# A fourth buffer for two tiles' rows of x, and one weight split moved up, in a fused attention and mixture-of-experts kernel

## The chip, the cores and the metric

The kernel runs on one core of a Trainium2 chip. The metric is the device time of one launch in microseconds (us), as the median of the runs shown; lower is better. A profiled execution, with the time of each instruction, stands beside it.

## The reference

Chunked softmax attention first (8 batches, 8 heads, 576 positions, heads of 64, chunks of 64 positions that see only themselves), then a mixture of 8 experts on its output. A token takes the expert that is the argmax of its gate, or, where its local gate is at 0.5 or above, the expert of the token before it:

```python
def _attn_ref(q, k, v):
    B, H, S, D = q.shape                      # 8, 8, 576, 64
    chunk = 64
    nc = S // chunk
    scale = 1.0 / np.sqrt(D)
...
    scores = scale * np.matmul(q_c, k_c.transpose(0, 1, 2, 4, 3))
    scores = scores - np.max(scores, axis=-1, keepdims=True)
    attn = np.exp(scores)
    attn = attn / (np.sum(attn, axis=-1, keepdims=True) + 1e-09)
    out = np.matmul(attn, v_c)
...
def _moe_ref(x, w_gate, w_local, w1, w2):     # w1: 8 x 512 x 1024, w2: 8 x 1024 x 512
    logits = np.einsum('bsd,de->bse', x, w_gate)
    local_gate = 1.0 / (1.0 + np.exp(-np.einsum('bsd,de->bse', x, w_local).squeeze(-1)))
...
            fresh_e = int(np.argmax(logits[b, s]))
            if s == 0 or local_gate[b, s] < 0.5:
                e = fresh_e
            else:
                e = prev_e if prev_e >= 0 else fresh_e
...
            p = np.exp(ls)
            p /= p.sum() + 1e-09
            h = np.maximum(x[b, s] @ w1[e], 0.0)
            out[b, s] = p[e] * (h @ w2[e])
```

x is the attention output with its heads side by side: 4608 tokens of 512.

## The kernel before

**Tiles.** The 4608 tokens are cut into 18 attention tiles of 256 (numbers 0 to 17). A tile goes through these steps: its q and k are loaded by DMA (buffers `qt`, `kt`, three of each; L135) and v (`vbuf`, three buffers until tile 11; L149); GpSimd (POOL) pairs the heads (`qr`, `kr`; L166); TensorE (PE) transposes the pairs into `qT`, `kT` (L174; ScalarE, ACT, copies them out of PSUM, L164); PE makes the scores (`sc`, L204), VectorE (DVE) takes the maximum off (L215, L218), ACT the exponential (`pr`, L223); PE transposes the result to `pT` and multiplies with v (`o`, L253); DVE divides by the sum and writes the rows of x into a buffer `xs` (L267, in two halves). PE transposes `xs` (L174, ACT copies to `xT`, L164) and makes the router's logits (`lg`, L296), which DVE copies (`lT`), PE transposes (L307, L309) and DVE reduces into the last columns of `xs` (L316). Then one DMA (L318) stores the tile from `xs` to `x_d` in DRAM. `xs` comes from a ring of three buffers, so the L267 that starts a tile waits until the store of the tile three before has read its buffer.

**The order.** It is written by hand. A steady loop runs i from 1 to 15 by a string of tokens, each engine in the order in which the instructions are recorded: iteration i has the scores of tile i+1, the transposes of `pr` and the values of tiles i and i-1, the q and k transposes of tile i+2, the pairs of tile i+3 on POOL, the x transposes, the router and the store of tile i-2, and the loads of q and k of tile i+5 and of v of tile i+2. SyncE's queue (SP) issues all loads and the stores to `x_d`, in order, and waits there for what a transfer needs. Behind the loop the last attention tiles are mixed with the first routed ones, and then the experts' matmuls follow.

**The first expert's weights.** w1 of an expert lies in four pieces of 128 x 1024, w2 in four pieces of 128 x 2 x 512. Each is loaded raw (`raw1` in the two buffers `raw_0`, `raw_1`; `raw2` in two more, `pair2[0]` and `pair2[1]`) and then split into a high and a low part: ACT casts to `w1h` (L102), then the low part `w1l` is raw minus high (L103), in this stage on POOL, in two halves of 512 columns. Piece c of w1 is loaded at the end of iteration 9+c and split at the end of iteration 11+c; the four pieces of w2 are loaded at the ends of iterations 13 and 14. Until then the first half of `pair2[0]` is unused, and `pair2[1]` serves as the third buffer of v.

**The first routed tiles.** Behind iteration 14, POOL writes the masks `rh` (L441) from DVE's running counts (L416 to L437, L819), and indirect DMAs (L613) gather the rows of the first experts' tiles into `raw_0` and `raw_1`; PE transposes them (L607) among the last attention tiles.

Of the kernel before, what the change touches and what calls it, by code (L numbers as in the profile page):

```python
# [8 lines left out]
F32 = mybir.dt.float32  # L9
# [12 lines left out]
E, F = 8, 1024  # L22
C = H * D
N = B * S
P = 128
NT = N // P
NS = N // 256
XR = C + E + 1
# [38 lines left out]
def tile_attention_then_moe(ctx: ExitStack, tc, q, k_in, v, wg, wl, w1, w2, out):  # L67
    nc = tc.nc
# [17 lines left out]
    w1h = [wpool.tile([P, F], F32R, name=f"w1h{c}") for c in range(4)]  # L86
    w1l = [wpool.tile([P, F], F32R, name=f"w1l{c}") for c in range(4)]
# [3 lines left out]
    pair2 = [wpool.tile([P, 4, C], F32, name=f"raw2_{g}") for g in range(2)]  # L91
    raw1 = [pair1[c // 2][:, c % 2] for c in range(4)]
    raw2 = [pair2[c // 2][:, c % 2 * 2:c % 2 * 2 + 2] for c in range(4)]

    def load_w1(e, c):
        nc.sync.dma_start(raw1[c], w1[e, P * c:P * c + P, :])

    def load_w2(e, c):
        nc.sync.dma_start(raw2[c], w2[e, 256 * c:256 * c + 256, :].rearrange("(f p) d -> p f d", p=P))

    def split(hi, lo, raw, lo_eng=None):
        nc.scalar.copy(hi, raw)  # L102
        (lo_eng or nc.vector).tensor_tensor(lo, raw, hi.bitcast(F32), ALU.subtract)  # L103
# [5 lines left out]
    pa2 = ctx.enter_context(tc.tile_pool(name="pa2", bufs=2, side="right"))  # L109
# [8 lines left out]
    vbuf = [pa1.tile([P, 2, H, DV], F32, name=f"v{i}") for i in range(2)]  # L118
    vbuf.append(pair2[1].rearrange("p a c -> p (a c)")[:, 0:2 * H * DV].rearrange("p (c h d) -> p c h d", c=2, h=H))
    V3 = 12  # L120

    def cut(i):
        n = -256 * i % S
        return 1 if n == 0 or n >= 256 else 2 if n == 128 else 4
# [16 lines left out]
    def load_v(i):  # L141
        vt = vbuf[i % 3 if i < V3 else i % 2]
        for cp in range(2):
            t0 = 256 * i + P * cp
            while t0 < 256 * i + P * cp + P:
                b, s0 = t0 // S, t0 % S
                n = min(S - s0, 256 * i + P * cp + P - t0)
                p0 = t0 % P
                nc.sync.dma_start(vt[p0:p0 + n, cp, :, 0:D], v[b, :, s0:s0 + n, :].rearrange("h s d -> s h d"))  # L149
                t0 += n  # L150
        return vt
# [92 lines left out]
    def values(pT, vt, xs, fine=False):  # L244
        box = {}

        def group(j, h):
            if h == 0:
                box["o"] = ps_o.tile([P, 2, 512], F32, name="o")
            o = box["o"]  # L250
            for cp in range(2):
                for cc in range(2):
                    nc.tensor.matmul(  # L253
                        o[64 * cp:64 * cp + 64, cc, DV * h:DV * h + D + 1],
                        pT[64 * cc:64 * cc + 64, 4 * j + h, 64 * cp:64 * cp + 64],
                        vt[64 * cc:64 * cc + 64, cp, 4 * j + h, 0:D + 1],
                        start=True, stop=True,
                    )
            if h == 3 and not fine:
                norm(j)  # L260

        def norm(j):
                ov = box["o"][:, :, 0:4 * DV].rearrange("p c (h d) -> p c h d", d=DV)
                rs = pa2.tile([P, 2, 4], F32, name="rs")
                nc.vector.tensor_scalar_add(rs, ov[:, :, :, D], 1e-9)
                nc.vector.reciprocal(rs, rs)
                nc.vector.tensor_tensor(  # L267
                    xs[:, :, 256 * j:256 * j + 256].rearrange("p c (h d) -> p c h d", d=D),
                    ov[:, :, :, 0:D],
                    rs.unsqueeze(3).to_broadcast([P, 2, 4, D]),  # L270
                    ALU.mult,
                )

        out = []
        for j in range(2):
            out += [lambda j=j, h=h: group(j, h) for h in range(4)]
            if fine:
                out.append(lambda j=j: norm(j))
        return out
# [42 lines left out]
    def ok(i):  # L322
        return 0 <= i < NS

    def load_vs(i):
        for n in range(2 if i == 1 else i + 2 - (i > V3), (i + 2 if i < V3 else i + 1) + 1):
            vts[n] = load_v(n)
# [119 lines left out]
    qk, hd, vts, qkT, prs, pTs, xss, xTs = ({} for _ in range(8))  # L447

    def a_tq(i, engs=None):
        qkT[i] = (pe2.tile([P, 4, 256], F32, name="qT", bufs=1), pe2.tile([P, 4, 256], F32, name="kT", bufs=1))  # L450
        return qk_transposes(hd.pop(i), *qkT[i], cut(i), engs)

    def a_pair(i, engs=(nc.gpsimd,) * 4):
        hd[i], fns = pair_heads(qk.pop(i), engs)
        return fns

    def a_sa(i, fine=False):
        prs[i] = pa2.tile([P, H, 2, D], F32, name="pr")
        return scores(*qkT.pop(i), prs[i], fine)

    def a_tp(i, fine=False):
        pTs[i] = pa2.tile([P, H, P], F32, name="pT")
        return p_transposes(prs.pop(i), pTs[i], fine)

    def a_va(i, fine=False):
        xss[i] = pa2.tile([P, 2, XR], F32, name="xs", bufs=3)
        return values(pTs.pop(i), vts.pop(i), xss[i], fine)

    def a_tx(i, fine=False):
        xTs[i] = pa2.tile([P, 4, 256], F32, name="xT", bufs=1)  # L470
        return x_transposes(xss[i], xTs[i], fine)

    def a_ra(i, fine=False):
        return router(i, xTs.pop(i), xss.pop(i), fine)

    def play(order, qs, its=None, more=False):
        its = {} if its is None else its
        for tok in order.split():
            name, _, n = tok.partition("*")
            if name not in its:  # L480
                its[name] = iter(qs[name]())
            for _ in range(int(n or 1)):
                next(its[name])()
        if more:
            return
        for name, it in its.items():
            assert next(it, None) is None, name
        assert set(its) == set(qs), set(qs) - set(its)

    def run(fns):  # L490
        for fn in fns:
            fn()
# [25 lines left out]
    for b in range(B):  # L518
        t, p = divmod(b * S, P)
# [11 lines left out]
    with tc.manual_schedule(engines=MAN):  # L531
        def load(store, fn, i):
            def go():
                store[i] = fn(i)
            return lambda: [go]
# [288 lines left out]
    hooks = {}  # L824
    for fn, at in zip(hq, PAR["hooks"]):
        hooks.setdefault(divmod(at, 4), []).append(fn)
    man = tc.manual_schedule(engines=MAN | {ET.Pool})
    man.__enter__()
    for i in range(1, NS - 2):
        qs4 = dict(s=lambda: a_sa(i + 1), tp=lambda: a_tp(i), va=lambda: a_va(i - 1, True), tq=lambda: a_tq(i + 2))  # L830
        opt = dict(lq=load(qk, load_qk, i + 5) if ok(i + 5) else None,
                   lv=(lambda: [lambda: load_vs(i)]),
                   pr=(lambda: a_pair(i + 3)) if ok(i + 3) else None, tx=(lambda: a_tx(i - 2)) if i >= 2 else None, ra=(lambda: a_ra(i - 2, True)) if i >= 2 else None)
        for h in range(4):
            opt[f"h{h}"] = (lambda h=h: [lambda: run(hooks[i, h])]) if (i, h) in hooks else None
        toks = [t for t in PAR["steady"].split() if opt.get(t.split("*")[0], 1) is not None]
        play(" ".join(toks), qs4 | {k: v for k, v in opt.items() if v is not None})
        if 9 <= i < 13:
            load_w1(0, i - 9)
        if i in (13, 14):  # L840
            for c in range(2 * i - 26, 2 * i - 24):
                load_w2(0, c)
        if 11 <= i < 15:
            for col in (slice(0, 512), slice(512, F)):
                split(w1h[i - 11][:, col], w1l[i - 11][:, col], raw1[i - 11][:, col], nc.gpsimd)

    def w2_split(c):
        return [lambda: nc.scalar.copy(w2h[c], raw2[c]),
# [4 lines left out]
    n = NS - 1  # L853
# [77 lines left out]
    for k, fn in (("tp", a_tp), ("va", a_va), ("tx", a_tx), ("ra", a_ra)):  # L931
        for d in range(5):
            queues[f"{k}{d}"] = lambda fn=fn, d=d: fn(n - d, True)
# [146 lines left out]
    with tc.manual_schedule(engines=MAN | {ET.SP, ET.Pool}):  # L1080
# [5 lines left out]
        for t in range(EARLY, LAST + 1):  # L1086
            step(t)
            n = t - EARLY
# [30 lines left out]
```

## Time and profile before

| | us |
|---|---|
| median of 3 runs | 672.22 (671.09 to 674.7) |
| profiled execution, whole | 675.2 |
| span of the profiled execution, first to last instruction | 673.4 |
| PE busy in the span | 633.6 |

The profiled execution took 675.2 us, of which 673.4 are the span in the trace. The program is 16385 instructions on five engines. The page's slices are 16.8 us each: PE is full from the tenth slice on, and short of full in the slices before, which are the attention stage.

### The profile page before, as it was taken

The page shows a single profiled execution, that of the slowest core. Times are in us where ns is not written, and L with a number is a line of the kernel's source. Part 1 is how long each engine was busy: PE and PEld are TensorE (multiplying, and loading weights), DVE is VectorE, ACT ScalarE, POOL GpSimd, SP SyncE. Part 2 cuts the span into 40 slices and gives each one's busy share as a digit, 9 for nine tenths or more (in the row PEclk, how much of TensorE's full clock was granted, in tenths as well). Part 3 has the DMA queues.
Part 4 walks back from the last instruction along what each step waited for, and adds up shares of the span by engine and source line. Part 5 has one row for each costly group of instructions (what it writes and reads, how often), then busy time and mean ns, then how long its engine had stood idle before and what let it go on. Part 6 is the DMA issues. An engine that isn't in the chain of part 4 may idle for free.

```text
span 673.4 us, 16385 instructions
## 1 busy us (share of the span) xinstructions
PE 633.6 (94%) x5684; PEld 503.2 (75%) x5684; DVE 362.6 (54%) x936; ACT 267.5 (40%) x439; POOL 150.8 (22%) x214
## 2 busy tenths in 40 slices
PE   5899989888999999999999999999999999999993
PEld 4677777666777887778888877788877888768872
DVE  2656667686787376663232466643467422564230
ACT  4657667656322235442122343422454222442220
POOL 5323224472022111211121121221122211212101
PEclk9989999998999999999999999999999999999998
DMA  9999999995614114545111153551148511244101
GB/s 230 249 229 258 236 264 280 301 282 164 236 37 143 33 49 174 177 160 177 35 64 34 33 191 145 191 172 44 38 171 292 176 38 34 66 158 167 48 19 37
DMA packets 102829, 98.23 MB, mean 146 GB/s; under 512 B 42388, under 2 KB 79252, under 8 KB 102676
## 3 DMA queue, kind: packets, MB, share of 16 engines
q1 hardware_dynamic: 88644, 61.01, 32.7%
q0 software_dynamic: 6640, 20.65, 9.2%
q10 hardware_dynamic: 7392, 14.68, 6.2%
q8 instruction: 77, 1.26, 0.8%
q14 instruction: 76, 0.62, 0.3%
HBM read 77.28 MB, written 20.35 MB: 145 GB/s over the span
## 4 chain that ended last, share of the span: by engine, by line
PE 39%; issue 26%; DMA 23%; DVE 5%; SPq 3%; POOL 2%; POOLq 1%; ACT 0%; DVEq 0%
DMA out<-ysb,sidx 14%; PE y L660 12%; PE h L646 12%; DMA x_d<-xs 7%; PE tr L174 4%; SPq L135 3%; PE o L253 2%; PE tr L740 2%; DVE xs L267 2%; PE tr L725 1%; PE y L667 1%; POOL rh L441 1%; DMA qt<-in_q 1%; PE h L654 1%; PE lg L296 1%
## 5 line engine op out<-in xcount | busy, mean ns | idle before, releaser
L660 PE MATMUL y<-w2h,hp 128*128 128x512 f32 x560 | 185.8, 401 | 1.0 <-ACTq L954 1.0
L646 PE MATMUL h<-w1h,xp 128*128 128x512 f32 x560 | 161.6, 398 | 0.0
L775 POOL DMA_INDIRECT out<-ysb,sidx x41 | 41.9, 1021 | 369.9 <-DVE ysb L772 284.3
L660 PEld LDWEIGHTS y<-w2h,hp 128*128 128x128 f32 x560 | 105.2, 188 | 24.8 <-ACTq L954 1.2
L646 PEld LDWEIGHTS h<-w1h,xp 128*128 128x128 f32 x560 | 102.1, 188 | 20.1 <-issue 0.2
L660 PE MATMUL y<-w2l,hp 128*128 128x512 f32 x280 | 110.7, 395 | 0.1
L646 PE MATMUL h<-w1l,xp 128*128 128x512 f32 x280 | 87.3, 393 | 0.4 <-DVEq L954 0.4
L713 ACT CAST hp<-tr 128x512 fp32r<-128x512 f32 x64 | 34.9, 589 | 119.5 <-PE tr L740 116.8
L772 DVE TENSOR_SCALAR ysb<-y,ppr 128x512 f32<-128x512 f32 x35 | 26.3, 750 | 87.4 <-PE y L660 68.1
L646 PEld LDWEIGHTS h<-w1l,xp 128*128 128x128 f32 x280 | 52.5, 188 | 12.4 <-DVEq L954 0.9
L660 PEld LDWEIGHTS y<-w2l,hp 128*128 128x128 f32 x280 | 52.7, 188 | 11.5 <-DVEq L954 0.6
L699 ACT ACTIVATE hsb<-h 128x1024 f32<-128x1024 f32 x35 | 35.9, 1026 | 60.2 <-PE h L646 57.6
L714 DVE TENSOR_TENSOR xp<-tr,xp 128x512 fp32r<-128x512 f32 x32 | 22.1, 690 | 58.9 <-ACTq L954 56.2
L714 DVE TENSOR_TENSOR hp<-tr,hp 128x512 fp32r<-128x512 f32 x64 | 41.6, 685 | 15.5 <-ACT hp L713 13.7
L632 ACT ACTIVATE pex<-pex 128x8 f32<-128x8 f32 x41 | 8.6, 209 | 102.4 <-DVE pex L631 89.1
L613 POOL DMA_INDIRECT xg<-x_d,gidx x39 | 41.4, 1063 | 14.1 <-issue 10.1
L740 PEld LDWEIGHTS tr<-ident,hsb 128*128 128x128 f32 x274 | 31.9, 140 | 9.0 <-ACTq L954 3.3
L740 PE MATMUL tr<-ident,hsb 128*128 128x128 f32 x274 | 37.3, 274 | 1.4 <-DVEq L954 1.4
L103 DVE TENSOR_TENSOR w1l<-raw,w1h 128x1024 fp32r<-128x1024 f32 x28 | 33.0, 1222 | 8.3 <-ACT w1h L102 8.3
L103 DVE TENSOR_TENSOR w2l<-raw,w2h 128x1024 fp32r<-128x1024 f32 x28 | 32.4, 1220 | 3.9 <-ACT w2h L102 3.9
L166 POOL COPY qr<-qt 128x512 f32<-128x512 f32 x34 | 19.9, 613 | 65.3 <-PE tr L174 44.0
L267 DVE TENSOR_TENSOR xs<-o,rs 128x512 f32<-128x512 f32 x36 | 24.9, 693 | 14.5 <-DMA x_d<-xs 13.6
(210 smaller groups left out, 851.5 us busy)
## 6 DMA issues: line engine op xcount, KB each, us to landing
raw<-in_moe_w SPq DMA_DIRECT2D x14, 1024.0 KB
raw<-in_moe_w ACTq DMA_DIRECT2D x14, 1024.0 KB, 6.4
x_d<-xs SPq DMA_DIRECT2D x18, 521.0 KB, 6.0
raw<-in_moe_w SPq DMA_DIRECT2D x16, 512.0 KB
v<-in_v SPq DMA_DIRECT2D x26, 256.0 KB, 7.0
qt<-in_q SPq DMA_DIRECT2D x11, 512.0 KB, 6.5
kt<-in_k SPq DMA_DIRECT2D x11, 512.0 KB, 7.6
qt<-in_q SPq DMA_DIRECT2D x16, 128.0 KB, 3.8
```

What stands on the lines that cost most here:

```text
L103: (lo_eng or nc.vector).tensor_tensor(lo, raw, hi.bitcast(F32), ALU.subtract)
L174: nc.tensor.transpose(box["ps"][:, n], src_of(n), ident)
L267: nc.vector.tensor_tensor(xs[:, :, 256 * j:256 * j + 256].rearrange("p c (h d) -> p c h d", d=D), ov[:, :, :, 0:D], rs.unsqueeze(3).to_bro ...
L613: nc.gpsimd.indirect_dma_start(out=dst, out_offset=None, in_=src, in_offset=bass.IndirectOffsetOnAxis(ap=gidx[t].bitcast(U32), axis=0))
L646: nc.tensor.matmul(hs[:, j], xs[a][:, c], W1[w][c][:, 512 * j:512 * j + 512], start=(c == 0 and n == 0), stop=(c == 3 and n == 2))
L660: nc.tensor.matmul(y, hx[f // 4][a][:, f % 4], W2[w][c][:, f % 2, :], start=(f == 0 and n == 0), stop=(f == 7 and n == 2))
L699: nc.scalar.activation(hsb, hs.rearrange("p j f -> p (j f)"), AF.Relu)
L713: nc.scalar.copy(p[:, 0], ps)
L714: V.tensor_tensor(p[:, 1], ps, p[:, 0].bitcast(F32), ALU.subtract)
L740: nc.tensor.transpose(ps[:, n], hsb[:, at + P * n:at + P * n + P], ident)
L772: either(kind and kind[1], lambda: V.tensor_scalar(ysb, y, pr, None, ALU.mult), lambda: y_part(ysb, y, pr))
L775: nc.gpsimd.indirect_dma_start(out=out, out_offset=bass.IndirectOffsetOnAxis(ap=sidx[t].bitcast(U32), axis=0), in_=ysb, in_offset=None, bo ...
```

## The change

Tiles 3 and 7 write their rows of x not into the ring but into a fourth place, `xs4`, which is the front of the raw w2 buffer `pair2[0]`; the ring of three then serves tiles 0, 1, 2, 4, 5, 6, 8, 9, 10, 11 and so on. The split of w1's piece 3 moves from the end of iteration 14 to the end of iteration 13, behind that of piece 2. The loads stand where they stood.

```diff
     V3 = 12
+    xs4 = pair2[0].rearrange("p a c -> p (a c)")[:, 0:2 * XR].rearrange("p (c n) -> p c n", c=2)
...
     def a_va(i, fine=False):
-        xss[i] = pa2.tile([P, 2, XR], F32, name="xs", bufs=3)
+        xss[i] = xs4 if i in (3, 7) else pa2.tile([P, 2, XR], F32, name="xs", bufs=3)
         return values(pTs.pop(i), vts.pop(i), xss[i], fine)
...
+    def w1_split(c):
+        for col in (slice(0, 512), slice(512, F)):
+            split(w1h[c][:, col], w1l[c][:, col], raw1[c][:, col], nc.gpsimd)
+
+    w1_at = {11: (0,), 12: (1,), 13: (2, 3)}
...
-        if 9 <= i < 13:
-            load_w1(0, i - 9)
+        for c in {9: (0,), 10: (1,), 11: (2,), 12: (3,)}.get(i, ()):
+            load_w1(0, c)
...
-        if 11 <= i < 15:
-            for col in (slice(0, 512), slice(512, F)):
-                split(w1h[i - 11][:, col], w1l[i - 11][:, col], raw1[i - 11][:, col], nc.gpsimd)
+        for c in w1_at.get(i, ()):
+            w1_split(c)
```

On ACT, at the border of iterations 13 and 14 (`w1h_75` and `w1h_76` are the high parts of pieces 2 and 3, `raw_1_90` the buffer of both raw pieces), the order of before is:

```order
82 L223 ACTIVATE pr<-pr 128x1024
83 L102 CAST w1h_75<-raw_1_90 128x512 x2
84 L164 COPY xT<-tr 128x8x64 x2
85 L164 COPY qT<-tr 128x512 x2
86 L164 COPY kT<-tr 128x512 x2
87 L164 COPY pT<-tr 128x512 x2
88 L223 ACTIVATE pr<-pr 128x1024
89 L102 CAST w1h_76<-raw_1_90 128x512 x2
90 L164 COPY xT<-tr 128x8x64 x2
```

and that of the change:

```order
82 L224 ACTIVATE pr<-pr 128x1024
83 L102 CAST w1h_75<-raw_1_90 128x512 x2
84 L102 CAST w1h_76<-raw_1_90 128x512 x2
85 L165 COPY xT<-tr 128x8x64 x2
86 L165 COPY qT<-tr 128x512 x2
87 L165 COPY kT<-tr 128x512 x2
88 L165 COPY pT<-tr 128x512 x2
89 L224 ACTIVATE pr<-pr 128x1024
90 L165 COPY xT<-tr 128x8x64 x2
```

The two casts of piece 3 now stand ahead of all of ACT's copies of iteration 14. Line numbers of the change are one higher from here on.

On POOL, at the same border and up to the first gathers, the order of before is (`w1l_79` and `w1l_80` are the low parts of pieces 2 and 3):

```order
67 L103 TENSOR_TENSOR w1l_79<-raw_1_90,w1h_75 128x512 x2
68 L166 COPY qr<-qt 128x4x128 x2
69 L166 COPY kr<-kt 128x4x128 x2
70 L441 TENSOR_SCALAR rh<-iota_m,rq 128x128 x12
71 L103 TENSOR_TENSOR w1l_80<-raw_1_90,w1h_76 128x512 x2
72 L613 DMA raw_0_89<-x_d,gidx_2952 128x521 x2
```

and that of the change:

```order
67 L103 TENSOR_TENSOR w1l_79<-raw_1_90,w1h_75 128x512 x2
68 L103 TENSOR_TENSOR w1l_80<-raw_1_90,w1h_76 128x512 x2
69 L167 COPY qr<-qt 128x4x128 x2
70 L167 COPY kr<-kt 128x4x128 x2
71 L442 TENSOR_SCALAR rh<-iota_m,rq 128x128 x12
72 L614 DMA raw_0_89<-x_d,gidx_2950 128x521 x2
```

The low part of piece 3 moves from behind the twelve masks to ahead of the pairs of tile 17. PE's, DVE's and SP's orders are the same, but for the buffer that tiles 3 and 7 name.

## Rows read from the trace of the kernel before

**Rows 1.** The page, part 2: busy tenths in 40 slices of the span.

```profile
PE   5899989888999999999999999999999999999993
DMA  9999999995614114545111153551148511244101
```

**Rows 2.** Waits of DVE from 45 to 131 us (total, times, longest).

```profile
DVE xs L267 <- DMA x_d<-xs: 13.6, 9, 2.5
```

**Rows 3.** DMA queues and issues, 20 to 140 us (KB each, median us to landing).

```profile
q1 hardware_dynamic: 62200, 31.15, 104.1%
...
kt<-in_k SPq DMA_DIRECT2D x9, 512.0 KB, 7.6
```

**Rows 4.** Timeline of SP's queue (start, duration, instruction [idle before, releaser]).

```profile
47.60 1.05 SPq L135 DMA_DIRECT2D kt<-in_k  x1
...
113.05 1.54 SPq L318 DMA_DIRECT2D x_d<-xs  x1
...
121.99 1.58 SPq L318 DMA_DIRECT2D x_d<-xs  x1
...
129.18 0.55 SPq L96 DMA_DIRECT2D raw<-in_moe_w  x1
129.82 2.28 SPq L149 DMA_DIRECT2D v<-in_v  x2
```

**Rows 5.** Timeline of DVE, 103 to 129 us.

```profile
104.03 0.22 DVE L316 TENSOR_REDUCE L<-lg 128x18 f32<-128x72 f32 x1
...
119.06 0.69 DVE L267 TENSOR_TENSOR xs<-o,rs 128x512 f32<-128x512 f32 x1 [1.87 <-DMA x_d<-xs]
...
128.31 0.69 DVE L267 TENSOR_TENSOR xs<-o,rs 128x512 f32<-128x512 f32 x1 [2.23 <-DMA x_d<-xs]
```

**Rows 6.** DMA issues from 130 to 133 us.

```profile
v<-in_v SPq DMA_DIRECT2D x2, 256.0 KB, 7.8
```

**Rows 7.** Timeline of ACT, 132 to 137 us.

```profile
132.77 1.14 ACT L102 CAST w1h<-raw 128x512 fp32r<-128x512 f32 x2
133.81 1.07 ACT L164 COPY xT<-tr 128x512 f32<-128x512 f32 x2
135.78 1.17 ACT L164 COPY qT<-tr 128x512 f32<-128x512 f32 x2 [0.90 <-PE tr L174]
```

**Rows 8.** Timeline of PE, 135 to 161 us.

```profile
135.03 1.09 PE L174 MATMUL tr<-ident,qr 128*128 128x128 f32 x8
136.06 0.64 PE L296 MATMUL lg<-xT,wg 128*32 128x256 f32 x8
...
147.69 0.70 PE L253 MATMUL o<-v,pT 64*64 64x65 f32 x32 [2.29 <-DVE xs L267]
...
159.24 0.77 PE L253 MATMUL o<-v,pT 64*64 64x65 f32 x32 [2.64 <-DVE xs L267]
...
160.21 1.06 PE L607 MATMUL tr<-ident,raw 128*128 128x128 f32 x4
```

**Rows 9.** Busy time by stretch: engines, then PEclk, DMA share, GB/s.

```profile
84.00:88.00 4.00, 2.12 (x46) 1.85 (x44) 2.46 (x7) 1.11 (x3) 1.17 (x2) 1.00 1.14 299
...
148.00:152.00 4.00, 3.68 (x62) 2.92 (x56) 3.86 (x11) 0.63 (x2) 4.00 (x6) 0.68 1.05 307
138.00:152.00 14.00, 11.38 (x238) 9.11 (x230) 12.89 (x45) 7.46 (x15) 10.27 (x16) 0.91 1.04 279
```

**Rows 10.** Timeline of POOL around the piece 3 subtraction, and an early pair copy.

```profile
60.06 1.17 POOL L166 COPY kr<-kt 128x512 f32<-128x512 f32 x2 [0.42 <-POOL qr L166]
...
136.25 1.17 POOL L166 COPY qr<-qt 128x512 f32<-128x512 f32 x2 [0.28 <-POOL w1l L103]
...
149.84 2.49 POOL L103 TENSOR_TENSOR w1l<-raw,w1h 128x512 fp32r<-128x512 f32 x2
```

**Rows 11.** Timeline of DVE: L579 beside the POOL subtraction, and later.

```profile
150.55 1.80 DVE L579 SCALAR_TENSOR_TENSOR id<-inv 128x3 f32<-128x3 f32 x1
...
201.04 0.17 DVE L579 SCALAR_TENSOR_TENSOR id<-inv 128x5 f32<-128x5 f32 x1
```

## The prediction

> **What bounds the kernel now.** The page's slices come first. PE is full from the tenth slice on, from some 160 us, and DMA has mostly ones to fives there; in the first nine slices it is the other way round, DMA at 9 throughout and PE at 8 or 9 [rows 1]. So the expert stage is PE's, and whatever delays its start is paid in full, while the attention stage, the only one that the change touches, has its limit elsewhere. The waits of DVE say where the first edit aims: L267, which writes the rows of x, stood 13.6 us in nine waits for stores that read its buffer [rows 2]. The other half of the picture is the queue that carries those stores. Its packets alone took 104.1% of the sixteen engines' time from 20 to 140 us [rows 3], and the timeline shows how far it lags: the rows of tile 8 were complete at 104.03 + 0.22 [rows 5], yet SP issued their store at 113.05 [rows 4], 9 us later. It was not waiting for data; it had not come to it. The store landed in time for DVE at 119.06, where tile 11's L267 had waited 1.87 for it, and the next one, issued at 121.99, released tile 12 at 128.31 after a wait of 2.23 [rows 4, 5]. The queue, not the ring, paces this stage.
>
> **Edit 1, the fourth place.** It adds no instruction and no byte. With tiles 3 and 7 out of the ring, tile 3 waits for nothing, tiles 4 to 10 wait for a store one tile older than before, and tiles 11 and 12 wait for those of 8 and 9, as before. The nine waits are those of tiles 4 to 12; the two that stay are 1.87 + 2.23 = 4.10 us long, so 13.6 - 4.1 = 9.5 us of seven waits are what the edit can remove. What is it worth? Compute would run ahead of the queue. But SP's order is unchanged and SP had a backlog at tile 8, so that the store at 113.05 and with it the landing at 119.06 don't come earlier because x was ready earlier: a lead that compute has gained is handed back as a longer wait at tiles 11 and 12. I cost the edit at **0**. The lead is small besides: the k rows issued at 47.60 land a median 7.6 later, at 55.2 [rows 3, 4], and POOL copies them at 60.06 [rows 10], so that compute can run at most 60.06 - 55.2 = 4.9 us earlier before it stands at the loads instead. Bounds: 0 and, if the queue did move up, -4.9 us. I take 0, because the 9 us backlog is a row of the very store that decides.
>
> **Edit 2, the split of piece 3.** It removes and adds the same four instructions (two casts on ACT, two subtractions on POOL); only the place differs. The question is when piece 3 is there. SP issues its load at 129.18 [rows 4]. No row shows its landing, since the split of before came much later. The nearest rows bound it: the store ahead of it took 128.31 - 121.99 = 6.3 us to its waiter [rows 4, 5], the v loads issued right behind it, at 129.82, a median 7.8 [rows 4, 6]. That gives 129.18 + 6.3 = 135.5 and 129.82 + 7.8 = 137.6; I take the middle, 136.6. In the new order ACT comes to piece 3's casts when those of piece 2 are done, at 133.81, where `xT` started in the kernel before [rows 7]. So ACT would stand from 133.81 to 136.6, cast until 136.6 + 1.14 = 137.7, and only then copy `xT`, 1.07 long, until 138.8. PE's logits, which read `xT`, started at 136.06 [rows 8] and would start at about 138.9: **+2.85 us** (1.75 and 3.85 with the bounds of the landing). ACT had 0.90 of idle ahead of `qT` [rows 7], but that is behind `xT` and doesn't help the logits. Queued behind ACT's wait are also `qT`, `kT` and `pT` of the iteration, and PE, which waits for the PSUM buffers that they empty.
>
> Is that shift absorbed further on? From 138 to 152 us DVE is busy 12.89 of 14 [rows 9], with the router's reduction, the counts and the masks in one row of steps that begins with the logits, and PE stands 2.29 us at 147.69 waiting for DVE's xs [rows 8]. So the DVE chain is the path there, it starts with the late logits, and it has 1.1 us of slack in all, spread over its hand-overs. The cast that is gone from the end of iteration 14 frees ACT 1.14 us where DVE sets the pace: **0**.
>
> The moved subtraction does three more things. POOL's qr copies of tile 17, at 136.25 [rows 10], come behind it, by some 2.5 us of subtraction plus ACT's wait; PE takes them an iteration later, which covers it. POOL no longer has the 2.49 us at 149.84 [rows 10] between the masks and the gathers. And DVE's L579, which took 1.80 us at 150.55 beside that subtraction but 0.17 at 201.04 [rows 11], should be short again: 1.63 us earlier indices. PE's first use of the gathered rows, at 160.21, however follows matmuls at 159.24 that waited 2.64 for DVE's xs, not for a gather [rows 8]: **0**, at most -1.6 if that wait should itself hang on L579.
> The Trainium skill's page "SBUF — State Buffer", section "Who interferes with whom", has a rule for L579: a DVE instruction with two SBUF inputs and a GpSimd one that reads SBUF exclude each other for a whole instruction. The trace agrees, 1.80 against 0.17; by that rule taken as time on the path the sum would be 1.63 us lower.
>
> **The clock.** New idle time of PE has a price of its own. After 2.29 us of waiting at 147.69 [rows 8], PE's granted clock is 0.68 over 148 to 152, that is part of it at the lower level of 1.2 GHz instead of 2.4; in 84 to 88, with PE busy 2.12 of 4, it stayed 1.00 [rows 9]. At 0.68 the 3.68 us of busy time would have been about 3.68 x 0.68 = 2.5 at full clock, so a fall costs up to 1.2 us. The new gap (some 2.85 us) is nearer to the first of these rows, but the slowed matmuls lie where DVE paces: half, **+0.6** (0 to 1.2).
> The Trainium skill's page "TensorE: Matmul & The Clock Gate", section "HAM oscillation — how this bites in real kernels", says that waits between bursts of matmuls drop the clock and make the next burst start slow. It speaks against this change; the sum by it has +1.2 where mine has +0.6, without it 0.
>
> **Sum.** 0 + 2.85 + 0.6 = +3.45 us. The profiled execution, at 675.2, gives 678.65; it lies 2.98 above the median of 672.22, so in terms of the median **675.7**. About 0.5%, 3.36 us, is what a measurement of this kernel can tell from no change: 675.58 and 668.86 are the borders.
>
> **The rivals.**
> A, the forecast: 674.0 to 677.4, with the bounds of the landing and the clock (1.75 + 0 and 3.85 + 1.2, each in from the corner by little). Chance 0.52.
> B, nothing comes of it. Either piece 3 has landed by 133.8, because the queue moves up with compute by some 2.8 us, or the stall is taken up before 160 us, where PE stood 2.64 at 159.24 [rows 8] and could stand less. For it: the queue follows compute somewhere ahead of 113 in ways that I have not seen. Against it: the 9 us backlog. 671.5 to 673. Chance 0.20.
> C, faster: DMA's full slices are an effect of waiting stores, not a limit; the queue moves up with compute, tiles 11 and 12 find their stores landed, and piece 3 is there when ACT asks. The lead is kept up to 4.9 us and costs the cast of 1.14 at the worst place: 672.22 - 4.9 + 1.14 = 668.5; with the waits of tiles 11 and 12 gone as well (4.1) 664.4. It decides from the point at which the store of tile 8 is issued 3 us or more before 113. For it: packet shares above 100% count overlap and don't prove that nothing more fits. Against it: the same backlog. 664.4 to 670.5. Chance 0.14.
> D, slower still: piece 3 lands later than 137.6, since compute's earlier loads crowd in front of it, or PE stays at the low clock into the routed tiles. The upper bounds, 3.85 + 1.2, give 677.3; a landing 2 us later 679.3. 677.4 to 680. Chance 0.12. Something else 0.02.
>
> **How the numbers follow.** A puts more than half of its chance above 675.58 (0.29), the rest within 0.5%; B is within; C is faster but for its upper end (0.12 and 0.02); D is slower. Faster 0.12, same 0.47, slower 0.41. The range reaches down through B to the upper part of C and up into D: 669.5 to 678.5, which leaves out the lower half of C (0.07) and most of D (0.08).
>
> **What would show it.** ACT's first cast of piece 3 in an idle wait of about 2.8 us for the load, with logits near 138.9 on the old time scale, and PE idle there; waits of tiles 4 to 10 for x_d near 0, and those of tiles 11 and 12 longer by the lead, with the store of tile 8 still issued near 113; L579 at about 0.17; the granted clock below 1 after the new gap. The prediction is wrong if the store of tile 8 is issued clearly earlier (C), or if the casts find piece 3 landed (B).

## The result, and the profile after

| | us |
|---|---|
| before, median of 15 runs | 672.7 (670.47 to 676.53) |
| changed, median of 15 runs | 677.77 (675.03 to 680.1) |
| ratio | 1.0067, 95% interval 1.0051 to 1.0083 |
| profiled execution of the changed kernel, whole / span | 677.03 / 675.0 |

The change made the kernel slower: by 0.67% or about 4.5 us by the ratio, which is used below, and by 5.07 us between the two medians. The executions of one kernel spread over 5 to 6 us, more than the effect, so the two profiles show where things moved and the ratios say what they are worth. The two profiled executions, 675.2 and 677.03, are only 1.8 us apart. The waits of DVE from 45 to 131 us in the changed kernel answer to [rows 2]:

```profile
DVE xs L268 <- DMA x_d<-xs: 4.0, 1, 4.0
```

Nine waits of 13.6 us have become one of 4.0. Most of this is not a lead: in the same stretch DVE's waits for PE's scores and values (`sc`, `o`) grew from 9.5 and 3.4 us to 11.9 and 8.8. The timelines of DVE and of SP's queue show where it is (they answer to [rows 5] and [rows 4]):

```profile
102.58 0.22 DVE L317 TENSOR_REDUCE L<-lg 128x18 f32<-128x72 f32 x1
...
120.69 0.69 DVE L268 TENSOR_TENSOR xs<-o,rs 128x512 f32<-128x512 f32 x1 [4.01 <-DMA x_d<-xs]
...
155.50 0.16 DVE L580 SCALAR_TENSOR_TENSOR id<-inv 128x3 f32<-128x3 f32 x1
```

```profile
114.32 1.07 SPq L319 DMA_DIRECT2D x_d<-xs  x1
...
130.74 0.74 SPq L96 DMA_DIRECT2D raw<-in_moe_w  x1
```

The last reduction of tile 8 began at 102.58, 1.45 us earlier than before, although that of tile 1 had begun 1.05 later in this execution (48.01 against 46.96). So compute had gained 2.5 us. The store of tile 8 was issued at 114.32 all the same, 11.5 us after its data, where it had been 8.8: SP's backlog grew by what compute had gained. Tile 11 then waited 4.01 instead of 1.87, and was later than before, at 120.69.

ACT's timeline at the border of iterations 13 and 14 (it answers to [rows 7]):

```profile
135.47 1.14 ACT L102 CAST w1h<-raw 128x512 fp32r<-128x512 f32 x2
138.70 1.14 ACT L102 CAST w1h<-raw 128x512 fp32r<-128x512 f32 x2 [2.09 <-DMA raw<-in_moe_w]
139.74 1.06 ACT L165 COPY xT<-tr 128x512 f32<-128x512 f32 x2
```

The casts of piece 3 waited 2.09 us for their load, and `xT` stood behind both: 2.09 + 1.14 = 3.2 us. PE's timeline (it answers to [rows 8]):

```profile
121.44 1.15 PE L254 MATMUL o<-raw,pT 64*64 64x65 f32 x32 [3.16 <-DVE xs L268]
...
140.46 0.63 PE L175 MATMUL tr<-ident,qr 128*128 128x128 f32 x4 [1.53 <-ACT xT L165]
141.02 0.64 PE L297 MATMUL lg<-xT,wg 128*32 128x256 f32 x8
...
161.94 0.70 PE L254 MATMUL o<-v,pT 64*64 64x65 f32 x32 [0.32 <-DVE xs L268]
...
162.73 0.60 PE L608 MATMUL tr<-ident,raw 128*128 128x128 f32 x4
```

The second half of the qr transposes waited for `xT` to empty a PSUM buffer, and the logits began at 141.02, 4.96 later than before. Not all of that is the wait's: the first half of these transposes had begun at 138.28, 3.25 later than before [rows 8], and only the other 1.71 stand between it and the logits. At 161.94 the wait of 2.64 for DVE's xs is down to 0.32, and the first gathered rows were transposed at 162.73, 2.5 later than before: in these two executions half of the 4.96 had been taken up by then. Last, the granted clock by stretch (columns as in [rows 9]):

```profile
120.00:124.00 4.00, 2.56 (x39) 2.44 (x40) 3.24 (x10) 0.00 (x0) 0.00 (x0) 0.60 1.09 289
124.00:128.00 4.00, 4.00 (x78) 3.49 (x77) 1.18 (x6) 3.15 (x5) 0.50 (x1) 0.55 1.24 273
...
140.00:144.00 4.00, 3.54 (x60) 2.75 (x61) 1.17 (x5) 3.06 (x6) 4.00 (x6) 1.00 0.99 302
...
156.00:160.00 4.00, 4.00 (x85) 3.21 (x83) 2.13 (x9) 2.71 (x4) 2.34 (x3) 0.71 1.01 297
```

Behind the long wait at tile 11 PE's granted clock was 0.60 and 0.55, most of these stretches at the level of 1.2 GHz, where it had been 1.00 before. It stayed 1.00 behind the new gap at 140.

### The profile page after: what moved, and what is told of

The parts are those of the page before. It is cut to its first block, busy times and chain, and to the rows that moved or that the text cites. A ratio compares the mean times of both kernels' runs of the same rounds, so it can differ in the third digit from the quotient of the medians.

```text
span 675.0 us, 16409 instructions
## 1 busy us (share of the span) xinstructions
PE 634.3 (94%) x5684; PEld 504.8 (75%) x5684; DVE 361.9 (54%) x936; ACT 268.2 (40%) x439; POOL 149.7 (22%) x214
## 4 chain that ended last, share of the span: by engine, by line
issue 25%; PE 17%; DMA 14%; POOLq 1%; POOL 0%; DVE 0%; DVEq 0%
DMA out<-ysb,sidx 14%; PE y L661 7%; PE h L647 7%; PE tr L741 1%; PE tr L726 1%; PE y L668 1%; POOLq L952 0%; PE h L655 0%; POOL xg L614 0%; POOLq L1121 0%; POOLq L776 0%; POOLq L1003 0%; POOL out L776 0%; DVE hf L167 0%; POOLq L614 0%
## 5 line engine op out<-in xcount | busy, mean ns | idle before, releaser
L661 PEld LDWEIGHTS y<-w2l,hp 128*128 128x128 f32 x280 | 52.8, 189 | 11.5 <-DVEq L960 0.8
L216 DVE TENSOR_REDUCE mx<-sc 128x8 f32<-128x512 f32 x36 | 23.2, 686 | 20.8 <-PE sc L205 20.8
```

The lines of the kernel that those rows point to most:

```text
L216: nc.vector.tensor_reduce(mxs[a], sc.rearrange("p j h c k -> p (j h c) k")[:, a:b], AX.X, ALU.max)
L661: nc.tensor.matmul(y, hx[f // 4][a][:, f % 4], W2[w][c][:, f % 2, :], start=(f == 0 and n == 0), stop=(f == 7 and n == 2))
```

## The experiments

Two questions stood: which of the two edits costs the 4.5 us, and by what. Theory 1 is that of the forecast: the first edit's lead is handed back to SP's queue and is worth nothing, and the second makes ACT wait ahead of `xT` for a load that is not there. Theory 2 came out of the profile after: the handed-back lead is one long wait, behind which PE's clock falls, so the first edit costs the larger part. Theory 3: the lead is worth something, and the second edit eats it. Each ratio is to runs of the kernel before on the same chip; one per cent is 6.7 us. Diffs are against the changed kernel unless said otherwise.

**Edit 1 alone.**

```diff
-    w1_at = {11: (0,), 12: (1,), 13: (2, 3)}
+    w1_at = {11: (0,), 12: (1,), 13: (2,), 14: (3,)}
```

> Edit 1 alone: tiles 3 and 7 in the fourth place, the split of piece 3 back at the end of iteration 14. Theory 1 (the forecast: the lead is handed back at tile 11, and the cost lies in the split): within 1 us of the kernel before. Theory 2 (from the profile after: the hand-back is one wait of about 4 us where two of about 2 stood, PE stands 3 us in one piece and its granted clock falls to 0.6 behind it): +1 to +3 us, with the wait of 4 us at tile 11 and the low clock at 120 to 128 us in the profile. Theory 3 (the lead is worth something and the split eats it): 2 to 5 us faster.

Measured: 1.0003 (0.9981 to 1.0025). No difference. The timeline of DVE in its profile shows the hand-back in its plainest form:

```profile
122.33 0.69 DVE L268 TENSOR_TENSOR xs<-o,rs 128x512 f32<-128x512 f32 x1 [8.74 <-DMA x_d<-xs]
```

The last reduction of tile 8 began at 101.05 in this execution, and its store was issued at 115.95. Of the 8.74 us, 1.87 had been waited before, 3.6 are lead (DVE was ready at 113.59 instead of 117.19), and 3.3 come from a store that landed later than before (122.33 against 119.06). This execution was the slowest of its twelve. The clock of PE was 0.60 and 0.55 in 120 to 128 us, as in the changed kernel, and cost nothing that the ratio resolves. Theory 1 had this right; theory 3 falls, and of theory 2 the interval leaves only the lower end (up to 1.7 us).

**Edit 2 alone.**

```diff
-        xss[i] = xs4 if i in (3, 7) else pa2.tile([P, 2, XR], F32, name="xs", bufs=3)
+        xss[i] = xs4 if i in () else pa2.tile([P, 2, XR], F32, name="xs", bufs=3)
```

> Edit 2 alone: all tiles in the ring of three, piece 3's split behind piece 2's at the end of iteration 13. Theory 1: +2.5 to +4 us, with ACT waiting about 2 to 3 us for the load of piece 3 ahead of its first cast. Theory 2 (the larger part of the loss is edit 1's): +1 to +2.5 us. Theory 3: +4 to +8 us, since edit 1's lead is missing.

Measured: 1.0054 (1.0036 to 1.0072), 3.6 us. ACT and PE at the same place:

```profile
139.73 1.14 ACT L102 CAST w1h<-raw 128x512 fp32r<-128x512 f32 x2 [2.29 <-DMA raw<-in_moe_w]
140.78 1.07 ACT L165 COPY xT<-tr 128x512 f32<-128x512 f32 x2
```

```profile
141.50 0.63 PE L175 MATMUL tr<-ident,qr 128*128 128x128 f32 x4 [2.60 <-ACT xT L165]
```

Here piece 3 was issued at 132.42, so that the casts began 7.3 us behind its issue, and PE's clock did fall behind the gap, to 0.82 and 0.75 in 140 to 148 us:

```profile
140.00:144.00 4.00, 2.50 (x20) 1.95 (x21) 1.00 (x3) 2.89 (x7) 3.57 (x4) 0.82 1.04 309
144.00:148.00 4.00, 4.00 (x93) 3.39 (x94) 1.91 (x9) 2.28 (x5) 1.23 (x3) 0.75 0.50 153
```

The second edit accounts for the loss, within the intervals.

What the low clock did can be read here. The transposes of kr right behind the logits, and the masks, with which POOL's part of the routing begins, are the first two lines before, then the same two with the second edit alone:

```profile
136.77 1.03 PE L174 MATMUL tr<-ident,kr 128*128 128x128 f32 x8
142.83 7.04 POOL L441 TENSOR_SCALAR rh<-iota_m,rq 128x128 bf16<-128x128 bf16 x12 [3.73 <-DVE qsA L819]
```

```profile
142.84 1.91 PE L175 MATMUL tr<-ident,kr 128*128 128x128 f32 x8
150.23 7.07 POOL L442 TENSOR_SCALAR rh<-iota_m,rq 128x128 bf16<-128x128 bf16 x12 [4.18 <-DVE qsA L820]
```

The masks began 142.83 - 136.06 = 6.77 us behind the logits before, and 150.23 - 142.06 = 8.17 with the second edit alone: 1.4 us of low clock, on the way to the masks. In the changed kernel's execution, without the fall, it was 147.78 - 141.02 = 6.76.

**Both edits, piece 3 loaded one iteration earlier.**

```diff
-        for c in {9: (0,), 10: (1,), 11: (2,), 12: (3,)}.get(i, ()):
+        for c in {9: (0,), 10: (1,), 11: (2, 3)}.get(i, ()):
```

> Both edits, and the load of piece 3 issued one iteration earlier, at the end of iteration 11 behind that of piece 2. Theory 1 (ACT's wait for the load is the larger part of the loss): ACT does not wait ahead of piece 3's casts, 1.5 to 3 us below the changed kernel, and what stays above the kernel before is the cast's 1.14 and edit 1's part. If it is the cast's place and not the wait, within 1 us of the changed kernel. The 512 KB that move ahead in the queue delay the stores behind them by some 1.5 us: if those pace the stage, that much of the gain is lost.

Measured: 1.0008 (0.9990 to 1.0025). That is 4.0 us below the changed kernel, more than the 1.5 to 3 expected. The loss is gone, with the casts and the subtractions exactly where the changed kernel has them. ACT runs through:

```profile
134.48 2.17 ACT L102 CAST w1h<-raw 128x512 fp32r<-128x512 f32 x4
136.54 1.08 ACT L165 COPY xT<-tr 128x512 f32<-128x512 f32 x2
```

So the wait was the price, not the place of the casts (whose 1.14 us would be 0.17%, and is within the interval), nor the order on POOL.

**The second edit alone with a longer wait.** The diff is against the second edit alone.

```diff
-        for c in {9: (0,), 10: (1,), 11: (2,), 12: (3,)}.get(i, ()):
+        for c in {9: (0,), 10: (1,), 11: (2,), 13: (3,)}.get(i, ()):
```

> The second edit alone with a larger wait: piece 3's split at the end of iteration 13, its load issued one iteration later, at the end of iteration 13 ahead of w2's. The load then is issued some 5 to 7 us later than with the second edit alone. Theory 1 (the wait at this place is paid nearly in full, up to the 2.6 us that PE gives back later): +4 to +7 us on the second edit alone, so 8 to 11 above the kernel before. If the loss came from the cast's place or from POOL's order, and not from the wait: the same as the second edit alone, within 1 us.

Measured: 1.0127 (1.0100 to 1.0154), 8.6 us, in six runs. Its ACT:

```profile
142.08 1.14 ACT L102 CAST w1h<-raw 128x512 fp32r<-128x512 f32 x2 [6.54 <-DMA raw<-in_moe_w]
```

The wait is 6.54 - 2.29 = 4.25 us longer than with the second edit alone, and the time 1.27 - 0.54 = 0.73% or 4.9 us longer (2.7 to 7.1 by the two intervals). A wait at this place is paid in full, as far as that can tell.

**The split in the middle of iteration 14.** Against the second edit alone:

```diff
-    w1_at = {11: (0,), 12: (1,), 13: (2, 3)}
+    w1_at = {11: (0,), 12: (1,), 13: (2,)}
...
+        opt["w"] = (lambda: [lambda: w1_split(3)]) if i == 14 else None
-        toks = [t for t in PAR["steady"].split() if opt.get(t.split("*")[0], 1) is not None]
+        toks = [t for t in PAR["steady"].replace("tp*8", "w tp*8").split() if opt.get(t.split("*")[0], 1) is not None]
```

> The second edit alone, but piece 3's split stands in the middle of iteration 14, behind the copies of xT, qT and kT and ahead of pT, with no load moved. Theory 1 (the loss is the wait ahead of xT): piece 3 has landed or lands within 0.5 us when ACT comes to it, so within 1.5 us of the kernel before. If the loss came from the subtraction on POOL standing ahead of the masks: about as the second edit alone, +3 us or more.

Measured: 1.0015 (0.9998 to 1.0032). In its profile the casts of piece 3, behind `kT`, waited for no load:

```profile
141.23 1.15 ACT L102 CAST w1h<-raw 128x512 fp32r<-128x512 f32 x2
```

No load was moved, and POOL's subtraction still stands ahead of the masks, though now behind the pairs of tile 17; moving the casts behind the copies that PE waits for took away most of the loss.

**Three tiles in the fourth place.** Without the second edit; the store of tile 11 now reads the front of the first raw pair, so w2's pieces are loaded in the order 2, 3, 0, 1. Against edit 1 alone:

```diff
-        xss[i] = xs4 if i in (3, 7) else pa2.tile([P, 2, XR], F32, name="xs", bufs=3)
+        xss[i] = xs4 if i in (3, 7, 11) else pa2.tile([P, 2, XR], F32, name="xs", bufs=3)
...
-            for c in range(2 * i - 26, 2 * i - 24):
+            for c in range(28 - 2 * i, 30 - 2 * i):
```

> Edit 1 extended to tile 11, without edit 2: tiles 3, 7 and 11 in the fourth place, and the loads of the first expert's w2 in the order of pieces 2, 3, 0, 1, so that the store of tile 11 has read the front of the first raw pair before piece 0 lands there. No tile then waits for the store that was 9 us behind. Theory 1 (the queue paces the stage; loads would stop compute next): within 1.5 us of the kernel before, with the idle time of tile 11 moved to waits for q, k or v. Theory 2 (the harm of edit 1 is the one long wait at tile 11): the wait is gone, the granted clock stays at 1.00 in 120 to 128 us, 1 to 3 us below edit 1 alone. If the ring was the limit, 4 us or more faster than before.

Measured: 0.9985 (0.9965 to 1.0004). No wait for a store is left in DVE's list. The waits from 100 to 160 us show what came in its place:

```profile
ACT w1h L102 <- DMA raw<-in_moe_w: 5.3, 2, 2.9
...
POOL qr L167 <- DMA qt<-in_q: 4.6, 1, 4.6
```

The casts of two pieces of w1 now wait for their loads, and POOL for q: the same queue, met at other places. One of them is the place of the second edit: the qr transposes of iteration 14 began at 130.52, a lead of 4.5 us, then PE stood 2.16 for `xT` behind the casts of piece 2, the granted clock was 0.76 and 0.81 in the stretches from 132 to 140, and the masks began at 142.22, where they had begun at 142.83 before. So the lead that three tiles give is real at 130 us, and is spent there on the same kind of wait.

**Three tiles, and all splits of w1 one iteration later.** Against the kernel with three tiles:

```diff
-    w1_at = {11: (0,), 12: (1,), 13: (2,), 14: (3,)}
+    w1_at = {12: (0,), 13: (1,), 14: (2,), 15: (3,)}
```

> Tiles 3, 7 and 11 in the fourth place, as in the run with these three, and all four splits of w1 one iteration later (ends of iterations 12 to 15), where that run showed ACT waiting 2.4 and 2.9 us for the loads of two pieces. Theory 1 (with the store's wait gone, the next limit is the loads of the weights' pieces on ACT and of q on POOL, 4.6 us): the casts no longer wait, 1 to 3 us below that run, so 2 to 4 us below the kernel before. If q's load alone paces it: the same as that run. If the subtractions that now stand beside the gathers on POOL delay the first routed tiles: 1 to 3 us above it.

Measured: 0.9969 (0.9951 to 0.9988), 2.1 us faster than the kernel before. This is the lowest ratio found, but its interval overlaps those of the kernels told just before it and just after it. The casts wait for no load any more; the waits from 100 to 165 us name q and now v:

```profile
POOL qr L167 <- DMA qt<-in_q: 5.7, 2, 3.0
...
PE o L254 <- DMA v<-in_v: 4.8, 3, 2.7
```

**The late splits without the fourth place.** Against the kernel just told:

```diff
-        xss[i] = xs4 if i in (3, 7, 11) else pa2.tile([P, 2, XR], F32, name="xs", bufs=3)
+        xss[i] = xs4 if i in () else pa2.tile([P, 2, XR], F32, name="xs", bufs=3)
```

> The late splits (ends of iterations 12 to 15) without any fourth place: all tiles in the ring of three, w2's pieces loaded in the order 2, 3, 0, 1. Tells what of the 0.31% that the three places with late splits gained comes from the places. Theory 1 (in the kernel before no cast waits for its load, so later splits free nothing; the gain needs the places): within 0.15% of the kernel before. If the late splits alone make the gain: 0.2% to 0.4% faster.

Measured: 0.9981 (0.9959 to 1.0003). This lies between the two expectations and its interval touches both. How much of the 0.31% comes from the fourth place and how much from the later splits stays open. In the profiles the masks began at 138.16 with the fourth place and at 142.87 without it, against 142.83 before; this speaks for the place, but is one execution of each.

## Why the prediction was right

The forecast was +3.45 us and 675.7; the ratio says +4.5 (3.4 to 5.6 by its interval), 677.77 in medians that themselves stand 0.5 us higher. The median as it stands lies a little above case A, in the range of D; put on the forecast's scale, 672.22 x 1.0067 = 676.7, it lies in A, and A's mechanism is the one that came. D's condition was met in the letter, since piece 3 landed at 138.70, behind 137.6; but ACT was later as well, and its wait was no longer than forecast.

**Edit 1 at 0: right, and shown.** Alone it measured 0.03%. The seven waits went, the store of tile 8 was not issued earlier, and the lead came back as part of a wait at tile 11 (4.01 in the changed kernel, 8.74 alone). Over all profiles this store was issued at 112.88 to 116.34 in the five kernels without the fourth place and at 113.80 to 115.95 in the five with it. The forecast spoke of longer waits at tiles 11 and 12; it was tile 11 that took all of it, and tile 12 then found its store landed.

**Edit 2 at +2.85: right, and shown.** Alone it measured 3.6 us (2.4 to 4.8), with the clock's share in it. The landing of piece 3, the term without a row of its own, was forecast at 7.4 us behind its issue; the casts began 8.0 us behind it in the changed kernel and 7.3 with the second edit alone. Its lower bound was taken from the store issued at 121.99, which was not the nearest: another was issued at 126.43, and no wait shows when that one landed. ACT's wait, forecast at 2.8 us, was 2.09 and 2.29, because ACT itself came later. The wait as the cause is shown from three sides: with the load earlier the loss is gone, with the wait 4.25 us longer 4.9 us are added, and with the casts behind `kT` most of it is gone. The traces say the same: this is the time from the first qr transposes of iteration 14 on PE to the first mask on POOL, beside the price by the ratio (us).

| kernel | from, to | longer than before | by the ratio |
|---|---|---|---|
| before | 135.03, 142.83 | | |
| edit 1 alone | 139.07, 146.86 | 0.0 | 0.2 (-1.3 to 1.7) |
| both, load earlier | 138.07, 145.85 | 0.0 | 0.5 (-0.7 to 1.7) |
| split in the middle of 14 | 137.78, 146.56 | 1.0 | 1.0 (-0.1 to 2.2) |
| changed | 138.28, 147.78 | 1.7 | 4.5 (3.4 to 5.6) |
| edit 2 alone | 138.24, 150.23 | 4.2 | 3.6 (2.4 to 4.8) |
| edit 2, load later | 136.44, 153.16 | 8.9 | 8.6 (6.8 to 10.4) |

Only the changed kernel's one profiled execution lies below its price: in it the wait was the shortest and the clock did not fall.

**No give-back: right for the whole 2.6, open for less.** In the profile of the changed kernel PE's wait of 2.64 at 159.24 shrank to 0.32, which rival B had named. By the table the second edit alone delayed the masks by 4.2 us and cost at least 2.4, which leaves no room for a give-back of 2.6, but some for up to 1.8.

**The gathers at 0: not contradicted.** L579 became 0.16 as forecast, but its chain was late by the logits' delay, and the sum needed nothing of it; whether its 1.63 us came back is inside the 1.8 just named. The Trainium skill's page "SBUF — State Buffer", section "Who interferes with whom", by which a DVE instruction with two SBUF inputs and a GpSimd one that reads SBUF contend, is borne out: away from POOL's subtraction the same instruction took 0.16 where it had taken 1.80.

**The clock at +0.6: too small where it fell, 0 where it did not.** The new gap dropped PE's clock with the second edit alone (0.82 and 0.75) and not in the changed kernel (1.00), where the idle time of PE there was 1.53 us against 2.60. Where it fell it delayed the masks by 1.4 us, above the forecast's upper bound of 1.2: the forecast halved the price because DVE paces there, but the slowed matmuls stand ahead of DVE's steps, and DVE waited 2.43 us for PE's `o` there instead of 1.03 in the changed kernel. In how many of the changed kernel's runs it fell is not known, so that its share in the 4.5 stays open. Behind tile 11's wait, where it also fell, the run of edit 1 alone shows no loss that goes with it.

Rival C fails on its own condition, since the store of tile 8 was issued at 114.32 and not 3 us before 113. The chances were too cautious about the sign: 0.47 for no change that can be told, where the whole interval lies above 0.5%. What made the difference to the forecast's 0.52% is within the interval of the two edits and can't be put down to one term.

## What to carry to other kernels

A wait for a buffer is worth nothing while the transfer that frees it comes out of a queue that is itself behind: look how long the data of that transfer had been ready before it was issued (9 us here), and expect the lead in a longer wait at the first place that still depends on the queue. Work that is moved to an earlier place meets its load there: compare the landing with the moment at which the engine would come to it, and put it behind whatever the busy engines wait for. When a stage is bound by a queue, shift its consumers later or its loads earlier: the load one iteration earlier (1.0008) and the casts behind the copies (1.0015) each took back most of the loss. More buffers alone gained nothing that could be told (1.0003 with two tiles in the fourth place, 0.9985 with three).

## What the runs showed of the hardware that was not expected

The same load of 512 KB (piece 3 of w1) released its waiter 8.0, 7.3 and 5.2 us behind its issue (issued at 130.74, 132.42 and 136.84) in three kernels, with a DMA share of 0.88 to 1.13 in the stretches between.

Of two gaps of PE at the same place in the order, 2.60 us was followed by a granted clock of 0.82 and 0.75 in the next two stretches of 4 us, and 1.53 us by 1.00.

In five executions one of DVE's short instructions (`id<-inv` of L579, or `qeq<-qsA,iota_q`) met POOL's pair of subtractions for a piece of w1, and in each it ended within 0.1 us of the end of the second half: at 152.35 against 152.33 before, where it took 1.80 us, and at 156.46 against 156.39 with edit 1 alone, where it took 2.50. Away from such a pair the two took 0.16 to 0.36.
